# A fourth accumulator in two schemes of seven products, a new order of the products, and six transposes moved behind a branch

## The chip, the cores and the metric

The kernel runs on one core of one Trainium2 chip. The metric is device time in microseconds (us), the median of several executions. The core's engines are named as in the profile: PE (TensorE, matrix products; PEld is its weight loads), DVE (VectorE), ACT (ScalarE), POOL (GpSimd) and SP (SyncE, which starts most transfers). Each works through a queue of its own, and they wait for one another through semaphores.

## The reference

A retention layer over 4 batches, 8 heads, 768 steps and head width 64 gives x, 3072 rows of 512. A router then picks one of 8 experts for each row, and each expert is a two-layer network of its own:

```
state = gamma * state + outer(k_t, v_t);  y_t = scale * q_t @ state        # retention, per batch and head
x     = y as [3072, 512]
logits = x @ w_gate                                                         # [512, 8]
e(row) = argmax(logits);  gate(row) = softmax(logits)[e]
h      = relu(x[rows of e] @ w1[e])                                         # [512, 1024]
out[rows of e] = gate * (h @ w2[e])                                         # [1024, 512]
```

All of it is float32.

## The kernel before, in words

**Stages.** The retention runs first (to about 130 us), in 24 steps of 128 rows. Its output rows are transposed, stored to device memory (`x_d`) and routed on the way. Then come the experts, one after another. The first 256 rows of expert 0 are done ahead of the others, in what is called here the early pair; the rest of expert 0 and experts 1 to 7 are the jobs e = 0 to 7 of the loop at L898. The number of rows n that an expert has is known only at run time, so each job is a switch over 33 unrolled arms, one for each multiple of 8 rows from 256 to 512. An engine enters an arm by a branch and comes back from it by another. PE and ACT get a hint that lets the arm be fetched ahead (`fetch_ahead`, L411).

**Layer 1 of an expert** (`quarters1`, products at L303, for jobs 2 to 7) multiplies w1 and x by a scheme of seven products in place of eight (2 by 2 blocks of w1 and x). It needs four sums of the blocks of w1, S (`halves_of_w1`, four subtractions on POOL at L275, the third of them written over a block of w1 itself), and four sums of the blocks of x, T (`halves_of_x`, four on DVE at L289). A copy of one column of the last T on POOL (L947, `turn_of`) holds POOL's S back until T is made. `quarters1` runs two rounds; a round treats two output blocks f side by side and has seven slots of two products:

- P1 = A11 X11 in `ya`, which ACT copies out to m1 (L315);
- S2 T2 in `yb`; DVE adds m1 and writes u2 (L307);
- S1 T1 in `yc`;
- S3 T3, accumulated on `yb`, so that `yb` holds both; DVE adds m1 and writes u3, then adds u3 to `yc` for one block of h (H11);
- A12 X21 accumulated on `ya`, which ACT turns into the block H00;
- A22 T4 accumulated on `yb`; DVE adds m1 (H10);
- S4 X22 accumulated on `yc`; DVE adds u2 (H01).

A product that accumulates on a bank cannot start before the engine that reads the bank's earlier content has read it.

**Layer 2** of an expert does its rows from 256 on by plain products (`layer2`, L236, two banks of its own, tag "y"), and its first 256 rows by a second scheme of seven (`pair`, products at L349, four matrix instructions each). `pair` uses sums of h, `hs` (`halves_of_h`, DVE, L253 to L256), and sums of w2, `ws` (`halves_of_w`, POOL, L265, done for the next expert during layer 1). Its order is the same: P1 in `ya`, which ACT reads twice (L364) for m10 and m11, with the gates as factors; S2 T2 in `yb`, which DVE reads for u2 (L355); S1 T1 in `yc`; the hint; S3 T3 accumulated on `yb`, which DVE reads for u3; then the part o of `yc`; then the three accumulating products on `ya`, `yb` and `yc`. The last two parts are put off into the next arm (`rest`). In the early pair the operations at L253 and L254 are on DVE and those at L255 and L256 on POOL, and DVE does transposes between its parts (`some`, 4, 7 and 5 of them).

**The banks.** The accumulators of jobs are a fixed list of six banks, `six`; the early pair takes its own by tag. Banks 0 and 1 are `ya` of `quarters1`, 2 and 3 `yb`, 4 and 5 `yc`; `pair` uses 0, 4 and 5; `layer2` alternates between the two banks of tag "y".

**The transposes of x** (`turn`, L209) make the next expert's x ready on DVE: 16 per expert, each of 32 partitions x 512 elements. `quarters1` calls `spare()` between its products, and PLACES says how many transposes each call does. What is left is done after the arm, behind the branch: `turn(xsn, xTn, range(TC), range(sum(PLACES) if e > 1 else 0, Q * Q))`. At job 1 all 16 are there. After it DVE makes T, and POOL, once T is made, makes S, then scatters rows of the output (L392) and gathers those of the expert after next (L166). SP loads w1 and w2 of the expert after next (L150, L155), w2 when the pair is done.

The order on every engine is the order of the code: the experts lie in a manually scheduled region.

## Time and profile before

| what | value |
|---|---|
| median of 3 runs | 480.64 us (478.64 to 481.42) |
| the profiled execution's own time | 479.97 us |
| its span in the profile | 478.2 us |
| mean granted clock of PE | 0.988 of full speed |
| PE busy, instructions | 446.6 us, 3550 |
| DVE busy, instructions | 294.9 us, 666 |
| POOL busy, instructions | 245.8 us, 192 |
| ACT busy, instructions | 130.4 us, 313 |
| early pair, first product at | 151.0 us |
| layer 1 of expert 1, first product at | 178.72 us |
| layer 1 of experts 2 to 7, first product at | 222.74, 264.90, 308.99, 349.94, 393.12, 429.23 us |
| pairs of experts 1 to 7, first product at | 209.01, 251.52, 295.62, 336.01, 379.22, 417.14, 457.49 us |

How to read the views: a line of the timeline has the start in us from the span's start, the length in us, engine, code line, operation, output and inputs by the program's names (banks are `p`, `yp`, `ye`), partitions x elements, and the number of instructions merged. In square brackets stands the engine's idle time before it, and what ended it; "issue" means that the profile shows nothing it waited for. One float32 matrix instruction appears as two rows of PE, so a product of `pair` is 8 rows. A line of the list of waits has the waiting engine and line, the one waited for, us in total, times, and the longest. A line of the stretches has the window, its length, then busy us and instructions of PE, PEld, DVE, ACT and POOL, PE's granted clock, the busy share of the DMA engines, and GB/s moved. Line numbers are those of the kernel before; after the change, lines from 804 on stand one lower.

### The profile page before, as it was taken

How to read it: one execution, taken by the hardware profiler on the slowest of the kernel's cores; microseconds unless marked ns; L12 is line 12 of the kernel's file. 1: busy time of each engine (PE TensorE's matmuls, PEld its weight loads, DVE VectorE, ACT ScalarE, POOL GpSimd, SP SyncE). 2: the span in 40 equal slices, each digit the busy share in tenths (PEclk: the TensorE clock that was granted, in tenths of full speed). 3: DMA queues.
4: the chain of work that ended last, by engine and by line, in shares of the span. 5: the costliest groups of instructions: out<-in, count | busy, mean ns of one | idle time of the engine just before them, and what ended most of it. 6: DMA issues, size and time to landing. Idle time of an engine off the chain costs nothing.

```text
span 478.2 us, 9303 instructions
## 1 busy us (share of the span) xinstructions
PE 446.6 (93%) x3550; PEld 356.2 (74%) x3550; DVE 294.9 (62%) x666; ACT 130.4 (27%) x313; POOL 245.8 (51%) x192
## 2 busy tenths in 40 slices
PE   8999998899799999999999999979999989999992
PEld 4777777677568955558867995779699679689872
DVE  4468768788687892744782694358468638833410
ACT  2454453445222111210231131113113212213310
POOL 2763533440306151759848863890588188089111
PEclk9999998999999999999999999989999999999998
DMA  9999999997831199343613714260562416001001
GB/s 201 226 229 225 216 240 233 211 217 217 268 90 40 33 382 374 125 146 106 235 37 146 269 48 164 83 246 2 180 205 105 162 59 211 5 6 61 3 28 48
DMA packets 93538, 72.71 MB, mean 152 GB/s; under 512 B 53482, under 2 KB 78058, under 8 KB 93424
## 3 DMA queue, kind: packets, MB, share of 16 engines
q1 hardware_dynamic: 88160, 58.74, 43.6%
q0 software_dynamic: 5120, 12.60, 7.4%
q8 instruction: 47, 0.77, 0.7%
q14 instruction: 67, 0.55, 0.3%
q10 hardware_dynamic: 144, 0.05, 0.0%
HBM read 60.88 MB, written 14.68 MB: 158 GB/s over the span
## 4 chain that ended last, share of the span: by engine, by line
PE 79%; DVE 11%; issue 3%; ACT 2%; SPq 1%; DMA 1%; another core or an unknown queue 1%; POOL 0%; POOLq 0%; DVEq 0%; ACTq 0%
PE p L303 23%; PE p L349 15%; PE ye L236 14%; PE p L223 6%; PE y L558 4%; PE sc L526 3%; PE hp L223 3%; PE tr L473 2%; PE yp L349 2%; DVE am L528 2%; PE new L537 2%; PE y L554 1%; PE parts L589 1%; SPq L460 1%; DMA q<-in_q_dram 1%
## 5 line engine op out<-in xcount | busy, mean ns | idle before, releaser
L236 PE MATMUL ye<-w2t,hT 128*8 128x128 f32 (+6 forms) x496 | 66.7, 361 | 0.0
L236 PEld LDWEIGHTS ye<-w2t,hT 128*8 128x8 f32 (+6 forms) x496 | 32.3, 122 | 30.1 <-issue 27.5
L392 POOL DMA_INDIRECT out_dram<-o,dst x30 | 29.9, 997 | 42.5 <-ACT o L244 14.7
L209 DVE STREAM_TRANSPOSE xT<-xs 32x512 f32<-32x512 f32 x64 | 44.9, 702 | 5.8 <-issue 4.7
L166 POOL DMA_INDIRECT xs<-x_d,src x28 | 29.3, 1047 | 29.5 <-DVE gate_e L201 17.1
L349 PE MATMUL p<-ws,hs 128*128 128x256 f32 x168 | 38.7, 382 | 5.3 <-DVE q L355 4.7
L528 DVE TENSOR_TENSOR am<-sc,causal 128x512 f32<-128x512 f32 x48 | 30.7, 682 | 18.5 <-PE sc L526 15.0
L209 DVE STREAM_TRANSPOSE xTs<-xs 32x512 f32<-32x512 f32 x48 | 33.7, 702 | 13.1 <-ACT hT L225 9.1
L303 PE MATMUL p<-t,w1t 128*128 128x196 f32 (+5 forms) x192 | 36.9, 335 | 3.8 <-DVE q L307 3.8
L349 PEld LDWEIGHTS p<-ws,hs 128*128 128x128 f32 x168 | 31.4, 190 | 11.6 <-POOL s L275 2.9
L490 POOL TENSOR_TENSOR vs<-v,dec 128x512 f32<-128x512 f32 x23 | 23.9, 1044 | 28.9 <-PE y L558 12.1
L485 POOL TENSOR_TENSOR qs<-q,dec 128x512 f32<-128x512 f32 x22 | 22.5, 1045 | 29.8 <-DMA q<-in_q_dram 28.8
L303 PEld LDWEIGHTS p<-t,w1t 128*128 128x128 f32 x192 | 32.8, 193 | 4.9 <-DVE q L307 2.7
L947 POOL COPY turn_of<-t 128x1 f32<-128x1 f32 x6 | 1.1, 183 | 68.4 <-DVE t L289 68.4
L355 DVE SCALAR_TENSOR_TENSOR q<-p,gate,q 128x256 f32<-128x256 f32 x14 | 6.8, 483 | 44.9 <-ACT q L364 26.9
L303 PE MATMUL p<-t,s 128*128 128x196 f32 (+5 forms) x192 | 33.8, 329 | 0.0
L265 POOL TENSOR_TENSOR ws<-w2t,ws 128x1024 f32<-128x1024 f32 x14 | 33.0, 2358 | 0.6
L265 POOL TENSOR_TENSOR ws<-w2t 128x1024 f32<-128x1024 f32 x14 | 33.1, 2364 | 0.1
L303 PEld LDWEIGHTS p<-t,s 128*128 128x128 f32 x192 | 32.1, 190 | 0.0
L307 DVE TENSOR_TENSOR hT<-p,q 128x196 f32<-128x196 f32 (+5 forms) x72 | 24.7, 360 | 10.4 <-PE p L303 8.9
L558 PE MATMUL y<-am,vs 128*64 128x128 f32 x384 | 29.3, 283 | 1.5 <-DVE am L528 1.1
L526 PE MATMUL sc<-qT,kT 64*128 64x128 f32 x384 | 28.8, 291 | 0.7 <-ACT kT L511 0.7
(204 smaller groups left out, 851.7 us busy)
## 6 DMA issues: line engine op xcount, KB each, us to landing
w1t<-in_moe_w_dram SPq DMA_DIRECT2D x8, 2048.0 KB, 8.0
w2t<-in_moe_w_dram SPq DMA_DIRECT2D x8, 2048.0 KB, 11.4
k<-in_k_dram SPq DMA_DIRECT2D x24, 256.0 KB, 5.5
v<-in_v_dram SPq DMA_DIRECT2D x24, 256.0 KB, 5.6
x_d<-xg SPq DMA_DIRECT2D x24, 256.0 KB, 4.9
q<-in_q_dram SPq DMA_DIRECT2D x11, 512.0 KB, 5.8
q<-in_q_dram SPq DMA_DIRECT2D x2, 256.0 KB, 3.6
out_dram<-o,dst POOLq DMA_INDIRECT x30, 3.7
```

Of the source, the lines that this page charges most:

```text
L166: nc.gpsimd.indirect_dma_start(out=xs[:, t, :], out_offset=None, in_=x_d[0:rows, :], in_offset=bass.IndirectOffsetOnAxis(ap=idx[:, t : t + ...
L209: nc.vector.transpose(xT[ts(g, L), :, 0 : n * P].rearrange("p a (t r i) -> p r t a i", r=Q, i=L)[:, r, :, :, :], xs[ts(r, L), tiles[0] : t ...
L223: nc.tensor.matmul(hp, lhsT=w1t[:, 0, dt, ts(f, P)], rhs=xT[:, dt, 0:n], start=(dt == 0), stop=(dt == DT - 1))
L236: nc.tensor.matmul(y[j * z : j * z + m, 0:c], lhsT=hT[:, f, t * P + r0 : t * P + r0 + m], rhs=w2t[:, 0, f, ts(j, c)], start=(i == 0), stop ...
L265: by.tensor_tensor(out=ws[i], in0=sums[i][0], in1=sums[i][1], op=ALU.subtract)
L303: nc.tensor.matmul(rows(y), lhsT=a(d, f), rhs=b(d), start=start and d == 0, stop=d == 1, skip_group_check=True)
L307: nc.vector.tensor_tensor(out=to, in0=rows(y), in1=rows(plus), op=ALU.add)
L349: nc.tensor.matmul(y, lhsT=a[:, f, :], rhs=b[:, f, :], start=start and f == 0, stop=f == FH - 1, skip_group_check=True)
L392: done = nc.gpsimd.indirect_dma_start(out=out[:, :], out_offset=bass.IndirectOffsetOnAxis(ap=idx[:, t : t + 1], axis=0), in_=o[:, t, :], i ...
L526: nc.tensor.matmul(sc[j][:, a, :], lhsT=kT[r, a, :], rhs=qT[r, a, :], start=True, stop=True)
L528: nc.vector.tensor_tensor(out=am[j], in0=sc[j], in1=middle(causal[:, :], HP), op=ALU.mult)
L558: nc.tensor.matmul(place_of(a, j), lhsT=vs[:, 2 * a + j, :], rhs=am[j][:, a, :], start=(c == 0), stop=True, skip_group_check=True)
```

## The change

- The list has eight banks now, `acc8`: the two of tag "y" come to it, and `layer2` is handed its bank from them in turn. `quarters1` now has `ya` in 6 and 7, `yb` in 0 and 1, `yc` in 2 and 3, `yd` in 4 and 5; `pair` has `ya`, `yb`, `yc` and `yd` in 4, 5, 2 and 3. The early pair takes a second bank of tag "y".
- Both schemes have a fourth accumulator, `yd`. S3 T3 starts there anew and is no longer added onto `yb`; u3 is then made from `yd` and u2 (in `pair`, from u21), and H10 from `yd` and u2. In `pair` u2 is made twice, once with each gate (u20, u21): six parts on DVE where there were five.
- S3 T3 comes third, ahead of S1 T1, in both schemes, so in the early pair as well. There u20 and u21 also come ahead of the four transposes that stood in front of u2.
- PLACES goes from 14 to 10 transposes per arm, with one `spare()` call moved; six of the sixteen transposes are behind the branch in place of two.

```diff
@@ -1,6 +1,6 @@
 import math
 from contextlib import ExitStack
-from itertools import chain
+from itertools import chain, cycle
 
 import numpy as np
 
@@ -215,21 +215,21 @@
         for _ in turns(xs, xT, tiles, which):
             pass
 
-    six = []
+    acc8 = []
 
     def layer1(n, xT, w1t, hT, f, tags=None):
-        hp = (ps(*tags[f % len(tags)], "hp") if tags else six[2 + f % 4])[:, 0:n]
+        hp = (ps(*tags[f % len(tags)], "hp") if tags else acc8[2 + f % 4])[:, 0:n]
         for dt in range(DT):
             nc.tensor.matmul(hp, lhsT=w1t[:, 0, dt, ts(f, P)], rhs=xT[:, dt, 0:n], start=(dt == 0),
                              stop=(dt == DT - 1))
         nc.scalar.activation(out=hT[:, f, 0:n], in_=hp, func=AF.Relu)
 
-    def layer2(n, hT, w2t, o, t, gate):
+    def layer2(n, hT, w2t, o, t, gate, turn_y):
 
         m = min(n - t * P, P)
         for r0, m in [(P // 2, m - P // 2), (0, P // 2)] if P // 2 < m <= P * 3 // 4 else [(0, m)]:
             parts = 4 if m <= P // 4 else 2 if m <= P // 2 else 1
-            y = ps("y", 2, "ye")
+            y = next(turn_y)
             c, z = DM // parts, P // parts
             for i, f in enumerate((0, 1, 4, 5, 6, 7, 2, 3)):
                 for j in range(parts):
@@ -308,7 +308,7 @@
 
         for f0 in range(0, FH, 2):
             fs = range(f0, f0 + 2)
-            ya, yb, yc = six[0:2], six[2:4], six[4:6]
+            ya, yb, yc, yd = (acc8[i : i + 2] for i in (6, 0, 2, 4))
             m1, u2, u3 = temps
             for i, f in enumerate(fs):
                 product(ya[i], A(0, 0), X(0, 0), f, True)
@@ -317,22 +317,22 @@
             for i, f in enumerate(fs):
                 product(yb[i], Sq(2), Tq(2), f, True)
                 add(rows(u2[i]), yb[i], m1[i])
+            spare()
+            for i, f in enumerate(fs):
+                product(yd[i], Sq(3), Tq(3), f, True)
+                add(rows(u3[i]), yd[i], u2[i])
+            spare()
             for i, f in enumerate(fs):
                 product(yc[i], Sq(1), Tq(1), f, True)
-            spare()
-            for i, f in enumerate(fs):
-                product(yb[i], Sq(3), Tq(3), f, False)
-                add(rows(u3[i]), yb[i], m1[i])
                 add(H(1, 1, f), yc[i], u3[i])
             spare()
             for i, f in enumerate(fs):
                 product(ya[i], A(0, 1), X(1, 0), f, False)
                 nc.scalar.activation(out=H(0, 0, f), in_=rows(ya[i]), func=AF.Relu)
             for i, f in enumerate(fs):
-                product(yb[i], A(1, 1), Tq(4), f, False)
-                add(H(1, 0, f), yb[i], m1[i])
+                product(yd[i], A(1, 1), Tq(4), f, False)
+                add(H(1, 0, f), yd[i], u2[i])
                 nc.scalar.activation(out=hT[:, FH + f, 0:n], in_=hT[:, FH + f, 0:n], func=AF.Relu)
-            spare()
             for i, f in enumerate(fs):
                 product(yc[i], Sq(4), X(1, 1), f, False)
                 add(H(0, 1, f), yc[i], u2[i])
@@ -341,7 +341,7 @@
     def pair(hT, w2t, hs, ws, o, gate, then, tile_of, spare=lambda n: None, tags=None,
              late=False):
 
-        ya, yb, yc = ((ps(*tag, "yp") if tags else six[tag])[:, 0:DH] for tag in tags or (0, 4, 5))
+        ya, yb, yc, yd = ((ps(*tag, "yp") if tags else acc8[tag])[:, 0:DH] for tag in tags or (4, 5, 2, 3))
         g = [gate[:, i : i + 1] for i in range(2)]
 
         def product(y, a, b, start):
@@ -363,27 +363,27 @@
         for i in range(2):
             nc.scalar.activation(out=m1[i], in_=ya, func=AF.Copy, scale=g[i])
         product(yb, S[2], T[2], True)
+        u20, u21 = (part(f"u2{i}", yb, i, m1[i]) for i in range(2))
         spare(4)
-        u2 = part("u2", yb, 0, m1[0])
+        product(yd, S[3], T[3], True)
+        u3 = part("u3", yd, 1, u21)
+        then()
+        spare(7)
         product(yc, S[1], T[1], True)
-        then()
-        product(yb, S[3], T[3], False)
-        spare(7)
-        u3 = part("u3", yb, 1, m1[1])
         part(o[:, 1, DH:DM], yc, 1, u3)
         spare(5)
         product(ya, A(0, 1), B(1, 0), False)
         nc.scalar.activation(out=o[:, 0, 0:DH], in_=ya, func=AF.Copy, scale=g[0])
-        product(yb, A(1, 1), T[4], False)
+        product(yd, A(1, 1), T[4], False)
         if not late:
-            part(o[:, 1, 0:DH], yb, 1, m1[1])
+            part(o[:, 1, 0:DH], yd, 1, u21)
         product(yc, S[4], B(1, 1), False)
         if not late:
-            part(o[:, 0, DH:DM], yc, 0, u2)
+            part(o[:, 0, DH:DM], yc, 0, u20)
 
         def rest():
-            part(o[:, 1, 0:DH], yb, 1, m1[1])
-            part(o[:, 0, DH:DM], yc, 0, u2)
+            part(o[:, 1, 0:DH], yd, 1, u21)
+            part(o[:, 0, DH:DM], yc, 0, u20)
 
         return rest
 
@@ -779,7 +779,7 @@
 
         pair(hTa, wa[1], S, T, oa, egates, lambda: fetch_ahead(which, 0),
              lambda name: att.tile([P, FH * P], F32, tag="v", name=name, bufs=6)[:, 0:DH], some,
-             (("sc", 2), ("sc", 2), ("y", 2)))
+             (("sc", 2), ("sc", 2), ("y", 2), ("y", 2)))
         scatter(oa, targets(*early, "_e"), range(HALF))
         turn(xs2[1], xT1, range(TC))
         dst = targets(inv, far, "")
@@ -800,11 +800,12 @@
 
         first(n)
         tiles = -(-n // P)
+        turn_y = cycle(acc8[6:8])
         order = [tiles - 1] * (tiles > first_tile) + list(range(first_tile, tiles - 1))
         for i, t in enumerate(order):
             if i + 1 == len(order):
                 then()
-            layer2(n, hT, w2t, o, t, gate)
+            layer2(n, hT, w2t, o, t, gate, turn_y)
         if not order:
             then()
 
@@ -860,7 +861,7 @@
                 nc.vector.tensor_tensor(out=val[:, :, i, :], in0=at, in1=inner(told[:, :, i], OV * TC), op=ALU.mult)
             here = mp.tile([P, NT, P], BF16, tag="hT", name="ohere")
             nc.vector.tensor_tensor(out=here, in0=middle(rrow[:, :], NT), in1=inner(prow[:, :], P), op=ALU.is_equal)
-            found = six[5][:, 0 : 5 * OV * TC]
+            found = acc8[5][:, 0 : 5 * OV * TC]
             for n in range(NT):
                 nc.tensor.matmul(found, lhsT=here[:, n, :], rhs=val[:, n, :, :].rearrange("p a s -> p (a s)"),
                                  start=(n == 0), stop=(n == NT - 1))
@@ -878,13 +879,13 @@
             for f in range(FT):
                 layer1(W, xT, w1t, hT, f)
             for t in range(TC):
-                layer2(W, hT, w2t, o2[E % 2], t, ogates[:, ts(j, TC)])
+                layer2(W, hT, w2t, o2[E % 2], t, ogates[:, ts(j, TC)], iter(acc8[6 + t % 2 : 7 + t % 2]))
             scatter(o2[E % 2], odst[:, ts(j, TC)], range(TC))
 
     with tc.manual_schedule(engines={PE, ACT, POOL, DVE, SP}):
         for t in o2:
             nc.gpsimd.memset(t, 0.0)
-        six.extend(ps(tag, n, f"p{i}") for i, (tag, n) in enumerate((("sc", 2), ("sc", 2), ("lg", 1)) + (("tr", 3),) * 3))
+        acc8.extend(ps(tag, n, f"p{i}") for i, (tag, n) in enumerate((("sc", 2), ("sc", 2), ("lg", 1)) + (("tr", 3),) * 3 + (("y", 2),) * 2))
         xT, xTn, rest = xTa, xT1, None
         s3 = [keep2.tile([P, 2, F // 2], F32, tag=f"s{i}", name=f"s{i}", bufs=1) for i in range(3)]
         T = [keep2.tile([P, 2, W // 2], F32, tag=f"t{i}", name=f"t{i}", bufs=1) for i in range(4)]
@@ -892,8 +893,8 @@
         ws = [keep2.tile([P, FH * DH], F32, tag=f"ws{i}", name=f"ws{i}", bufs=1) for i in range(4)]
         temps = [[keep2.tile([P, W // 2], F32, tag=f"q{k}{i}", name=f"q{k}{i}", bufs=1) for i in range(2)] for k in range(3)]
         turn_of = keep2.tile([P, 1], F32, tag="turn_of", name="turn_of", bufs=1)
-        of_pair = dict(m10=temps[0][0], m11=temps[0][1], u2=temps[1][0], u3=temps[2][0])
-        PLACES = (2, 2, 2, 1) * 2
+        of_pair = dict(m10=temps[0][0], m11=temps[0][1], u20=temps[1][0], u21=temps[1][1], u3=temps[2][0])
+        PLACES = (1, 1, 1, 2) * 2
 
         for e in range(E):
             last = e + 1 == E
```

## The prediction

> **What bounds the kernel now.** I read the page first: who is busy, and the chain of work that ended last.
>
> ```profile
> PE 446.6 (93%) x3550; PEld 356.2 (74%) x3550; DVE 294.9 (62%) x666; ACT 130.4 (27%) x313; POOL 245.8 (51%) x192
> ...
> PE 79%; DVE 11%; issue 3%; ACT 2%; SPq 1%; DMA 1%; another core or an unknown queue 1%; POOL 0%; POOLq 0%; DVEq 0%; ACTq 0%
> ```
>
> PE carries the span. The change adds no product and removes none, so it can only fill PE's idle time or make more of it. The second view is therefore the list of waits, PE's rows alone:
>
> ```profile
> PE p L349 <- DVE q L355: 4.7, 5, 1.1
> PE p L303 <- DVE q L307: 3.8, 4, 2.0
> ```
>
> L349 is the product of `pair`, L303 that of `quarters1`: both wait for DVE, nine times. The third view is the timeline of one such wait, in the pair of expert 2:
>
> ```profile
> 251.52 1.89 PE L349 MATMUL p<-w2t,hT 128*128 128x256 f32 x8
> ...
> 253.25 3.62 PE L349 MATMUL p<-ws,hs 128*128 128x256 f32 x16
> ...
> 256.78 0.84 ACT L364 ACTIVATE q<-p,gate 128x256 f32<-128x256 f32 x2 [4.37 <-issue]
> 257.29 0.48 DVE L355 SCALAR_TENSOR_TENSOR q<-p,gate,q 128x256 f32<-128x256 f32 x1 [4.28 <-ACT q L364]
> ...
> 257.92 1.97 PE L349 MATMUL p<-ws,hs 128*128 128x256 f32 x8 [1.06 <-DVE q L355]
> ```
>
> Three products run; the fourth accumulates on `yb`, which DVE must read first, with an operand that ACT, late from the branch, gives at 257.25. The pair of expert 6, where ACT is early, shows the undisturbed length:
>
> ```profile
> 417.14 1.89 PE L349 MATMUL p<-w2t,hT 128*128 128x256 f32 x8
> ...
> 418.87 5.34 PE L349 MATMUL p<-ws,hs 128*128 128x256 f32 x24
> ...
> 429.23 1.54 PE L303 MATMUL p<-xT,w1t 128*128 128x204 f32 x8
> ```
>
> First product to next expert: 12.09 us, 1.73 a product.
>
> **1. The pairs of experts 1 to 5.** By the same two rows they take 13.73, 13.38, 13.37, 13.93 and 13.90 us (209.01 to 222.74, 251.52 to 264.90, 295.62 to 308.99, 336.01 to 349.94, 379.22 to 393.12): 7.9 us above five times 12.09. Of this 1.9 stays: 0.8 at expert 1 (second product waits for the sums of h until 211.50 instead of 210.74), 0.6 at expert 4 (its weight loads wait for ACT 0.20 and 0.46) and 0.5 at expert 5 (the branch, idle 0.38 and a fresh start). The other 6.0 is the wait on `yb`. With `yd` the third product starts a bank of its own and the fourth is on `yc`; neither waits for DVE. What is late next: the fifth product needs ACT's two copies (end 6.10 us after the pair's start at expert 2; the fifth starts at 6.9), and the sixth needs DVE's u3. At expert 2: u20 from 257.29, then u21 and u3 at 0.5 each end by 258.8; the sixth starts at 251.52 + 5 x 1.73 = 260.2. The added DVE operation (six in place of five, 0.48) is in this. At expert 1 the third product now needs the last sum of h (L256, ends 212.68); it starts at 211.50 + 1.73 = 213.23. **-6.0**; ends -4.5 (ACT's return, 4.4 us after its last row, varies: 0.3 of it back at each expert) and -6.2 (only PE's idle times kept).
>
> **2. The six turns behind the branch.** Per expert 2 to 6 four more transposes follow the join: 4 x 0.72 = 2.9 us on DVE, ahead of the four L289 subtractions, POOL's L947 copy and four L275 subtractions, and the pair's own parts. Tightest is expert 4, whose layer 2 is shortest: L289 ends 340.26, now 343.1; u20, u21, u3 end by 344.7; the sixth product comes at 336.01 + 0.6 + 8.65 = 345.3. POOL's third subtraction (w1t, L275) ends 347.56, now 350.4, and the third product of the next layer 1 reads it: 336.01 + 0.6 + 12.09 = 348.7, plus two slots of 1.41, 351.5. It holds by 1.1; at expert 6 (427.19 + 2.9 against 429.23 + 2.8) by 1.9, elsewhere by over 3. So I cost it at nothing. Queued behind on POOL: two scatters, the gathers, the sums of the next w2 (done at 443.95 at expert 7, needed after 457). No DMA is added; gathers and scatters come 2.9 later.
>
> **3. quarters1.** By the chain of waits in order of time, layer 1 of experts 3 and 7 takes 20.07 us at 212 columns and 19.32 at 204: 0.0947 a column in both. At that rate experts 2, 4 and 5 (196, 176, 208 columns) lose 19.77 - 18.56 = 1.2, 21.55 - 16.67 = 4.9 and 20.32 - 19.70 = 0.6: 6.7 together. Expert 4:
>
> ```profile
> 310.26 2.55 PE L303 MATMUL p<-t,s 128*128 128x176 f32 x16
> ...
> 312.82 0.31 ACT L315 COPY q<-p 128x176 f32<-128x176 f32 x1 [2.51 <-PE p L303]
> ...
> 314.28 0.34 DVE L307 TENSOR_TENSOR q<-p,q 128x176 f32<-128x176 f32 x1 [3.39 <-issue]
> ...
> 314.76 0.83 PE L303 MATMUL p<-t,w1t 128*128 128x176 f32 x4 [1.95 <-DVE q L307]
> ```
>
> ACT and DVE are idle, yet start their reads 2 to 3 us after the rows of the products end: the word that a product is done comes late. The stretches of time show this core moving 320 GB/s there, and then:
>
> ```profile
> 312.90:316.30 3.40, 1.01 (x5) 0.78 (x6) 0.88 (x3) 0.22 (x1) 3.07 (x3) 1.00 0.96 320
> 316.40:319.80 3.40, 3.40 (x13) 3.40 (x13) 3.24 (x8) 0.32 (x1) 3.32 (x3) 0.50 0.89 339
> ```
>
> 3.4 us at half clock: 1.7 of expert 4's 4.9. Before, slot four (of seven, 1.4 us each) reads what DVE does with the first half of slot two: 1.5 slots less 0.6, so some 1.5 us of lateness are hidden. After, DVE's first claim is on slot six: u3, after two u2 adds, one transpose and its own add: 3 slots less 1.65, so 2.5 us. With the lateness as it is, expert 4 still waits some 2.4 (its ya, yb, yd and yc end about 314.9, u3 about 317.2) and keeps the half clock; it gains 0.6, experts 2 and 5 half of theirs, 0.9: 1.5 in all. But the lateness follows POOL's gathers (L166), which begin 4.9, 0.5, -2.3 and 2.5 us from the start of layer 1 of experts 2 to 5; with step 2, and pairs 1.2 shorter, they begin about 4 us later, and expert 4 comes to where expert 5 is now (loss 0.6): that gives 4.3 at expert 4 alone. I take **-2.9**, halfway, since neither row is nearer; ends 0 and -6.7. DVE has four transposes fewer in the branch (2.9 us of 20), which helps the same slots.
>
> A rule speaks against a part of this. The Trainium skill, "TensorE: Matmul & The Clock Gate", Part 1 (the clock gate), says that PE's clock falls to half after a whole idle window of about 3.4 us. Expert 4's waits are 1.95 and 0.52, so by the rule the spell is not their doing and stays when they go: its gain of 4.3 would be 2.6, and the sum below 473.2. In the rows the spell follows a stretch with PE busy 1.01 of 3.4 us, and the only earlier one (77.5 to 80.8) one with 1.84 of 3.4; I go by the rows.
>
> **4. The early pair (before the experts).** Here the third product ahead costs something.
>
> ```profile
> 153.18 5.42 PE L349 MATMUL yp<-we,he 128*128 128x256 f32 x24 [0.29 <-DVE he L254]
> ...
> 154.42 1.26 POOL L256 TENSOR_TENSOR he<-hTa 128x512 f32<-128x512 f32 x1
> 155.27 0.48 DVE L355 SCALAR_TENSOR_TENSOR u<-yp,gate_e,m 128x256 f32<-128x256 f32 x1 [0.54 <-PE yp L349]
> ```
>
> POOL makes the last sum of h, done at 155.68; as fourth operand it is wanted at 156.71, as third at 154.98. PE waits 0.75. DVE does worse: the four transposes that now lie at 152.95 to 154.73, in front of u, come behind u20 and u21. From 155.27: two parts 1.0, four transposes 1.8, u3 0.5, seven 3.1, the part of o 0.5, five 2.3, and the last two parts end at about 165.55, where the last L355 row (163.82, 0.48) now ends at 164.30: 1.25 later. Then follow, unmoved, eight small operations and sixteen transposes, which end at 178.5, and layer 1 of expert 1 starts at 178.72. It starts later by **+1.25**; ends +0.75 (PE's wait alone) and +1.5.
>
> **Sum.** -6.0 - 2.9 + 1.25 = -7.65, against the profiled execution's own 479.97 (span 478.2 and 1.8 around it): **472.3**. The 479.97 lies 0.7 below the median of the runs, 480.64; I leave the forecast as it is.
>
> **Rivals.** (a) Only the pairs gain: the late word comes as now and quarters1 returns 1.5 or less. For it: the lateness has its own cause. 479.97 - 6.0 - 1.5 + 1.25 = 473.7; with -4.5 from step 1 and nothing from quarters1, 476.7. (b) The change doesn't do what it says: the wait moves from the fourth to the fifth product, because ACT's copies come later than now. From 0.8 us later on each us costs one; 2 us later at five experts and the 6.0 is gone: 479 to 480. Against it: experts 1 and 6, where ACT came 2.6 us earlier. (c) Slower: the four moved turns, 2.9 us, come onto PE's path at the five joins of experts 2 to 6, over L289, POOL's L275 and the third product: 5 x 2.9 = 14.5, so 479.97 - 6.0 + 1.25 + 14.5 = 489.7. It decides where POOL's third subtraction ends over 1.1 us (expert 4), 1.9 (6) or 3 (others) later than I reckon. Against it: POOL's rows keep 2.34 to 2.37 whatever runs beside them.
>
> **How the numbers follow.** The forecast 0.55, (a) 0.27, (b) 0.08, (c) 0.05, and 0.05 for the unnamed. 0.5% is 2.4 us, about what measuring this kernel can tell from no change; faster means below 478.2. The forecast, (a) and little of the rest are faster: 0.85; (b) mostly the same: 0.09; slower 0.06. Low end: -6.0 - 6.7 + 1.25, 468.5; high end: the 476.7 of (a) and 0.9 for late signals that fall worse (half of what experts 2 and 5 lose now), 477.6.
>
> **What would show it.** The rows PE L349 <- DVE L355 gone, and pairs of 12.1 to 12.7 us; no new row PE <- ACT L364 at the fifth product; layer 1 near 0.0947 a column; the early pair's third product waiting for POOL about 0.7, and layer 1 of expert 1 starting near 180.0; L947 about 2.9 later against the pair. Wrong if PE's L303 waits for POOL L275, or if waits of L303 on L307 grow.

## The result and the profile after

The changed kernel takes 471.95 us (median of 6 runs, 471.41 to 474.16) where the kernel before, beside it, takes 479.87 (477.08 to 482.35): ratio 0.9843, 95% interval 0.9801 to 0.9885 (ratios here are taken over all the runs, so they are not exactly the quotient of the two medians). The forecast was 472.3. The profiled execution of the changed kernel was the slowest of its six: 474.16 us, with a span of 472.4, against 479.97 and 478.2 before.

The list of PE's waits of the changed kernel (total us, times, longest us) has no row of L349 for DVE L355 any more, and less of L303 for L307:

```profile
PE p L303 <- DVE q L307: 1.1, 2, 0.7
...
PE p L303 <- DVE hT L307: 0.7, 1, 0.7
```

The timeline of the pair of expert 2:

```profile
252.35 1.89 PE L349 MATMUL p<-w2t,hT 128*128 128x256 f32 x8
...
254.08 5.34 PE L349 MATMUL p<-ws,hs 128*128 128x256 f32 x24
...
257.66 0.84 ACT L364 ACTIVATE q<-p,gate 128x256 f32<-128x256 f32 x2 [4.42 <-issue]
...
258.17 1.46 DVE L355 SCALAR_TENSOR_TENSOR q<-p,gate,q 128x256 f32<-128x256 f32 x3 [0.45 <-ACT q L364]
...
259.26 1.89 PE L349 MATMUL p<-w2t,hT 128*128 128x256 f32 x8
...
264.44 1.60 PE L303 MATMUL p<-xT,w1t 128*128 128x212 f32 x8
```

ACT is as late as before (4.42), but PE runs through: 264.44 - 252.35 = 12.09 us in place of 13.38. The same subtraction of first rows, for every stage that moved:

| stage, us | before | after |
|---|---|---|
| early pair's start to layer 1 of expert 1 | 27.72 | 28.67 |
| pairs of experts 1, 2, 3, 4, 5 | 13.73, 13.38, 13.37, 13.93, 13.90 | 12.92, 12.09, 12.09, 12.59, 12.99 |
| layer 1 of experts 2, 3, 4, 5 | 19.87, 20.16, 21.54, 20.42 | 19.39, 20.16, 18.23, 20.81 |
| early pair's start to the end of the span | 327.2 | 320.6 |

The pairs give 5.6 us, layer 1 gives 3.4, the early pair takes 0.95; layer 2 takes 1.5 more, and the stages ahead of the early pair 0.8. In the early pair the third product now waits for POOL, as reckoned (timeline):

```profile
155.20 1.26 POOL L256 TENSOR_TENSOR he<-hTa 128x512 f32<-128x512 f32 x1
...
156.51 3.72 PE L349 MATMUL yp<-we,he 128*128 128x256 f32 x16 [0.58 <-POOL he L256]
```

The late word in layer 1 is still there. Expert 4 met it in the first of its rounds before, and meets it in the second now (timeline after):

```profile
317.98 1.36 PE L303 MATMUL p<-t,w1t 128*128 128x176 f32 x8
...
319.62 0.59 DVE L307 TENSOR_TENSOR hT<-p,q 128x176 f32<-128x176 f32 x2 [1.82 <-PE p L303]
...
320.02 1.46 PE L303 MATMUL p<-t,s 128*128 128x176 f32 x8 [0.68 <-DVE hT L307]
```

The spell of half clock that stood at 316.39 before is gone from expert 4. The lateness reaches into layer 2 now. Its first weight loads wait for ACT, which waits for the last sums of DVE (timeline after, expert 4):

```profile
325.75 1.09 DVE L307 TENSOR_TENSOR hT<-p,q 128x176 f32<-128x176 f32 x4
326.12 0.89 ACT L335 ACTIVATE hT<-hT 128x352 f32<-128x352 f32 x2 [3.10 <-DVE hT L307]
...
326.68 0.16 PEld L236 LDWEIGHTS p<-w2t,hT 128*32 128x32 f32 x8 [0.40 <-ACT hT L335]
```

Layer 2 of experts 2, 4 and 5, the ones that met the late word, takes 9.39, 6.03 and 9.42 us, where it took 8.91, 5.48 and 8.86 before (and takes 8.83, 5.49 and 8.86 in the changed kernel on chip B, see below, with no late word): 1.6 of layer 1's 3.4 us come back there.

So far the forecast held. The experiments ran on four other occasions, each on a chip of its own, which I call A, B, C and D. Which chip gave the first result is not on record; "the first chip" below means that occasion, and chip and occasion can't be told apart. On A, B and C the kernel before took 468.9, 468.5 and 468.7 us; on D, 476.95. In no profile of A to C is a late word found. The changed kernel itself ran again on B, and there **it is slower, by 0.5%**. What follows is mostly about that.

### The profile page after: what moved, and what is told of

Its sections match the earlier page's. It is cut to its first block, busy times and chain, and to the rows that moved or that the text cites. A ratio compares the mean times of both kernels' runs of the same rounds, so it can differ in the third digit from the quotient of the medians.

```text
span 472.4 us, 9372 instructions
## 1 busy us (share of the span) xinstructions
PE 447.4 (95%) x3550; PEld 356.0 (75%) x3550; DVE 301.1 (64%) x674; ACT 130.5 (28%) x313; POOL 245.8 (52%) x192
## 4 chain that ended last, share of the span: by engine, by line
PE 77%; DVE 15%; issue 2%; ACT 1%; SPq 1%; DMA 1%; POOL 1%; POOLq 0%; another core or an unknown queue 0%; DVEq 0%; ACTq 0%
PE p L303 21%; PE p L349 17%; PE p L236 12%; PE p L223 5%; PE y L558 4%; PE sc L526 4%; DVE xT L209 4%; PE hp L223 3%; PE tr L473 3%; PE new L537 2%; PE y L554 2%; PE parts L589 2%; DVE am L528 1%; DMA q<-in_q_dram 1%; DVE xTa L209 1%
## 5 line engine op out<-in xcount | busy, mean ns | idle before, releaser
L236 PE MATMUL p<-w2t,hT 128*8 128x128 f32 (+6 forms) x496 | 67.9, 362 | 0.3
L236 PEld LDWEIGHTS p<-w2t,hT 128*8 128x8 f32 (+6 forms) x496 | 31.7, 122 | 32.1 <-issue 27.2
L349 PE MATMUL p<-ws,hs 128*128 128x256 f32 x168 | 37.5, 379 | 0.6 <-DVE hs L254 0.6
L303 PE MATMUL p<-t,w1t 128*128 128x196 f32 (+5 forms) x192 | 36.1, 331 | 1.2 <-DVE q L307 1.1
L303 PE MATMUL p<-t,s 128*128 128x196 f32 (+5 forms) x192 | 35.9, 330 | 0.7 <-DVE hT L307 0.7
L349 PEld LDWEIGHTS p<-ws,hs 128*128 128x128 f32 x168 | 31.8, 190 | 5.3 <-issue 1.0
L948 POOL COPY turn_of<-t 128x1 f32<-128x1 f32 x6 | 1.1, 183 | 64.2 <-DVE t L289 64.2
L307 DVE TENSOR_TENSOR hT<-p,q 128x196 f32<-128x196 f32 (+5 forms) x72 | 23.9, 359 | 16.6 <-PE p L303 13.5
L303 PEld LDWEIGHTS p<-t,w1t 128*128 128x128 f32 x192 | 32.3, 190 | 2.1 <-DVE q L307 2.1
L265 POOL TENSOR_TENSOR ws<-w2t,ws 128x1024 f32<-128x1024 f32 x14 | 33.0, 2358 | 0.6
L265 POOL TENSOR_TENSOR ws<-w2t 128x1024 f32<-128x1024 f32 x14 | 33.1, 2364 | 0.1
L303 PEld LDWEIGHTS p<-t,s 128*128 128x128 f32 x192 | 32.4, 190 | 0.9 <-DVE hT L307 0.9
L558 PE MATMUL y<-am,vs 128*64 128x128 f32 x384 | 30.3, 287 | 2.4 <-DVE am L528 2.2
L307 DVE TENSOR_TENSOR q<-p,q 128x196 f32<-128x196 f32 (+5 forms) x48 | 16.2, 360 | 24.3 <-PE p L303 12.9
L355 DVE SCALAR_TENSOR_TENSOR o<-p,gate,q 128x256 f32<-128x256 f32 x21 | 10.0, 483 | 30.6 <-PE p L349 30.2
```

The source lines that it names most:

```text
L236: nc.tensor.matmul(y[j * z : j * z + m, 0:c], lhsT=hT[:, f, t * P + r0 : t * P + r0 + m], rhs=w2t[:, 0, f, ts(j, c)], start=(i == 0), stop ...
L265: by.tensor_tensor(out=ws[i], in0=sums[i][0], in1=sums[i][1], op=ALU.subtract)
L303: nc.tensor.matmul(rows(y), lhsT=a(d, f), rhs=b(d), start=start and d == 0, stop=d == 1, skip_group_check=True)
L307: nc.vector.tensor_tensor(out=to, in0=rows(y), in1=rows(plus), op=ALU.add)
L349: nc.tensor.matmul(y, lhsT=a[:, f, :], rhs=b[:, f, :], start=start and f == 0, stop=f == FH - 1, skip_group_check=True)
L558: nc.tensor.matmul(place_of(a, j), lhsT=vs[:, 2 * a + j, :], rhs=am[j][:, a, :], start=(c == 0), stop=True, skip_group_check=True)
```

## The experiments

Each time is a median beside the kernel before on the same chip, with the ratio to it and its 95% interval. "From the early pair on" is the span less the start of the early pair, from the profiled execution: what lies ahead of it is the same code in all kernels and differs by up to 4 us from one execution to the next (early pair at 144.9 to 148.8).

| kernel | chip | time, ratio | from the early pair on | pair of expert 4 |
|---|---|---|---|---|
| before, again (before_again) | B | 468.27 (one run) | 321.2 | 15.45 |
| changed, again (after_again) | B | 470.84, 1.0051 (1.003 to 1.0073) | 323.5 | 20.69 |
| x1: fourteen turns in the branch | A | 463.84, 0.9887 (0.9842 to 0.9932) | 315.7 | 12.58 |
| x2: before with the placing alone | A | 472.89, 1.0064 (1.0031 to 1.0097) | 325.6 | 16.49 |
| x3: old pairs | A | 470.81, 1.0043 (1.002 to 1.0066) | 323.5 | 13.18 |
| x4: old quarters1 | A | 470.28, 1.0026 (1.0 to 1.0053) | 322.0 | 19.33 |
| x5: old early pair | B | 469.76, 1.002 (0.9993 to 1.0046) | 322.5 | 20.25 |
| x11: before, w1 loaded late | B | 463.99, 0.9889 (0.9847 to 0.9931) | 315.7 | 13.55 |
| x9: sums of w2 first | C | 463.08, 0.987 (0.9825 to 0.9915) | 315.7 | 12.58 |
| x12: changed, w1 loaded late | C | 466.44, 0.9935 (0.9906 to 0.9963) | 319.7 | 16.42 |
| x15: all that helps | C | 460.69, 0.9822 (0.9787 to 0.9856) | 314.4 | 12.58 |
| x17: before with two moves | D | 470.87, 0.9887 (0.9843 to 0.993) | 319.3 | 12.58 |

### First four: parts undone, or done alone

The expected times of these four were reckoned for the first chip; on A the kernel before takes 11 us less, so stages and ratios are compared.

**x1.** The changed kernel with the old placing:

```diff
-        PLACES = (1, 1, 1, 2) * 2
+        PLACES = (2, 2, 2, 1) * 2
```

> The changed kernel with the turns of x placed as before: fourteen of the sixteen in the branch, two behind it. Theory (fourth accumulator does the work): the pairs of experts 2, 3 and 6 stay at 12.1 us and no L349 waits for DVE L355, so 5.6 us of the gain stay. Layer 1 loses somewhat more than its 3.3 us beside 0.0951 us a column, because scatter and gathers of POOL come 2.9 us earlier and their late stretch falls deeper into layer 1: 4 to 5.5 us lost, time 472.5 to 474.5. Rival (the placing of the turns is what helped layer 1): layer 1 of expert 4 goes back to 20.5 us or more, the 3.4 us are gone, time about 475.5.

Measured: no L349 waits for L355, pairs 12.09 at experts 2, 3 and 6, as the theory says. But layer 1 takes 18.66, 20.16, 16.80 and 19.79 us at experts 2 to 5: at 0.0951 us a column nothing is lost, and both sides' reckoning of a late word has no object here.

**x2.** The kernel before with `PLACES = (1, 1, 1, 2) * 2` and nothing else.

> The kernel before, with one edit: ten of the sixteen turns in the branch, six behind it. Three accumulators and the old order stay. Theory: the pairs keep their wait on yb; it is set by ACT's late copies, the two more transposes ahead of u2 lie in the time in which DVE waits for ACT, so experts 2 to 5 stay at 13.4 to 13.9 us, expert 6 (ACT early) grows by up to 1 us; layer 1 returns at most 1 to 2 of its 6.7 lost us because the late stretch moves by 2.9 us. Time 478 to 481. Rival (placing alone frees layer 1): layer 1 of expert 4 falls from 21.5 to near 18.2 us and the time to 476 to 477.

Measured: L349 waits for L355 six times, 6.9 us. Experts 2, 3 and 5 take 13.34, 13.22 and 14.34, expert 6 13.72 (12.09 in the kernel before), expert 4 16.49. Layer 1 is the same as in x1. The placing alone brings nothing here and costs; more at expert 6 (1.6) than the theory's 1, since u2 waits behind four further turns (six in place of two), not two as the expectation has it.

**x3.** The changed kernel with `pair` as before. Its first accumulator then lies on a bank that the last tile of layer 2 uses:

```diff
-        ya, yb, yc, yd = (... for tag in tags or (4, 5, 2, 3))
+        ya, yb, yc = (... for tag in tags or (6, 2, 3))
```

> The changed kernel with the function pair as before (three accumulators, third product on yc), early pair and those of the experts; quarters1 and the placing stay new. Theory: pairs of experts 1 to 5 back to 13.4 to 13.9 us (13.4 to 14.4 where four transposes ahead of u2 outlast ACT), +5.6 us; layer 1 of expert 1 starts 0.95 us earlier against the early pair; layer 1 as in the changed kernel, 19.4, 20.2, 18.2 and 20.8 us for experts 2 to 5. Time about 476.6 (475.8 to 478.5). Rival (most of the gain is layer 1's): under 474.5.

Measured: this bank brings a wait of its own, of L349 for ACT's L244, 4.7 us in six, and moves the pairs' start 0.94 later (expert 4's 1.7); so its single terms can't be read. Layer 2 and pair together, which hold the move, take 22.33 and 23.96 us at experts 2 and 3, against 20.92 and 22.65 in x1, which has also fewer turns behind the branch: 1.4 and 1.3 us, about what the fourth accumulator gave in the result, but the bank's wait is in them, so this is no separate proof. The total tells nothing, as expert 4 shows next.

**x4.** The changed kernel with the products of `quarters1` in the old order:

```diff
-            ya, yb, yc, yd = (acc8[i : i + 2] for i in (6, 0, 2, 4))
+            ya, yb, yc = acc8[6:8], acc8[0:2], acc8[2:4]
...
+                product(yb[i], Sq(3), Tq(3), f, False)
+                add(rows(u3[i]), yb[i], m1[i])
```

> The changed kernel with the order of quarters1 as before (its fourth product on yb, on banks that the pair's last products do not use); the pair and the placing stay new. Theory (yd lets layer 1 tolerate a late word by one slot more): the L303 waits for DVE L307 come back, experts 2 to 5 lose 5 to 7 us against 0.0951 a column in place of 3.3, time 473.5 to 475.4. Rival (layer 1 gained only because scatter and gathers come later): losses stay at 3 to 3.5 us and the time within 0.7 us of the changed kernel's 472.

Measured: layer 1 of experts 2 to 5 is the same to 0.01 us as in x1. Where no word is late, the old order and the new cost the same, so this run does not tell the two readings of layer 1's gain apart. But the pair of expert 4 takes 19.33 us, and it is the changed kernel's pair. Four kernels of the twelve have that pair at 16.4 to 20.7 us, with PE waiting at the sixth product: x4, x5, x12 and the changed kernel on B. (x2's 16.49 is another case: PE waits 1.98 us at the fourth product, as in the kernel before, behind ACT and the four further turns.)

### The same two kernels on chip B, and two parts

**The changed kernel again.**

> The changed kernel itself, beside the kernel before, on the chip of these runs, where the kernel before takes 468.9 us and not 479.9, and where no kernel shows the late word in layer 1 (expert 4's takes 16.80 us). Theory: with no late word only the pairs and the early pair are left of the change: -5.6 + 0.95, so about 464.2 us, and layer 1 as in the other kernels here (18.67, 20.16, 16.80 and 19.79 us for experts 2 to 5). It holds only if DVE leaves expert 4's branch early; if it leaves over 1 us after the load of w1 is issued, its return takes 4.5 us and not 1.5, and expert 4's pair grows by 5 to 7 us: then 469 to 471. Rival (the quarters' order and the placing bring their part on every chip): 461 or less.

**The kernel before again.**

> The kernel before, for its profile on the chip of these runs. Theory: layer 1 of experts 2 to 5 in 18.67, 20.16, 16.80 and 19.79 us, 6.5 us less than in its first profile; the pairs of experts 2 to 5 at 13.4 to 13.9 with the wait on DVE L355 as they were; the rest of the 11 us ahead of the early pair, which starts near 146 to 148 and not at 151. Rival (the pairs' wait is a thing of the first chip too): pairs of 12.1 here.

Measured: 470.84 for the changed kernel against 468.5. From the early pair on the kernel before has 321.2 us, the changed one 323.5. The pairs of experts 1 to 3 are shorter by 0.92, 1.13 and 1.28, that of 5 by 0.59; from the early pair to layer 1 of expert 1 it takes 1.13 longer (28.85 for 27.72); layer 1 is the same to 0.1; expert 4's pair takes 20.69 in place of 15.45. The case that the expectation set apart, DVE leaving expert 4's branch late, is what came. In the kernel before, layer 1 is 6.5 us shorter than in its first profile and the wait on L355 is there (4.9 us in five), both as expected: the wait belongs to the kernel, the late word to the first occasion.

**x5.** The changed kernel, with the early pair calling the old `pair`.

> The changed kernel with the early pair in its old order (third product on yc, three accumulators); the experts' pairs, quarters1 and the placing stay new. Theory: the wait of yp L349 for POOL's he goes, layer 1 of expert 1 starts 27.7 us after the early pair begins and not 28.7, and 0.95 us are gained against the changed kernel. Rival (DVE's queue, which is free again before layer 1 of expert 1, hides it): the same 28.7 us and no gain.

Measured: 28.03 us from the early pair to layer 1 of expert 1 against 28.85 in the changed kernel on this chip: 0.82 gained, 0.95 expected; the medians differ by 1.08. No slack of DVE hides it. Expert 4's pair stays long (20.25).

**x11.** The kernel before; the load of w1 moves in SyncE's queue:

```diff
-            if e + 2 < E:
-                w1s.append(weights1(homes[e % 2], e + 2))
...
             if e + 2 < E:
                 w2s.append(weights2(homes[e % 2], e + 2))
+                w1s.append(weights1(homes[e % 2], e + 2))
```

> The kernel before with one edit: the load of w1 for the expert after next is issued behind the load of w2 at the end of the job, 12 to 16 us later, not ahead of the pair. Theory (ACT is late from the branch because its first instructions behind it are fetched while the load of w1 moves; where ACT left within 0.7 us of the issue or no load ran it took 1.7 to 2.6 us, else 4.2 to 5.0): ACT's gap at experts 2 to 5 falls to 1.7 to 2.6 us, the wait of L349 for DVE L355 goes or falls under 0.4 us, pairs of experts 2 to 5 at 12.1 to 12.6 us without any fourth accumulator, time 464 to 465. Rival (ACT's return has another cause, as the length of its code): gaps stay at 4.2 to 5.0, pairs at 13.4 to 13.9, time as before.

Measured: as the theory says, with three accumulators. The pair of expert 2, timeline of the kernel before on chip B and then of this one:

```profile
249.56 0.84 ACT L364 ACTIVATE q<-p,gate 128x256 f32<-128x256 f32 x2 [4.21 <-issue]
...
250.69 1.97 PE L349 MATMUL p<-ws,hs 128*128 128x256 f32 x8 [0.89 <-DVE q L355]
```

```profile
249.72 5.34 PE L349 MATMUL p<-ws,hs 128*128 128x256 f32 x24
250.60 0.84 ACT L364 ACTIVATE q<-p,gate 128x256 f32<-128x256 f32 x2 [1.71 <-PE p L349]
...
260.89 0.42 SPq L150 DMA_DIRECT2D w1t<-in_moe_w_dram  x1
```

With the load out of the way ACT is idle 1.71 and not 4.21 us, the third and fourth product run on without a gap (x24), and experts 2, 3 and 5 take 12.09. The time is 463.99, at the low end of the 464 to 465 expected. One edit in another queue gives as much as the fourth accumulator does with fourteen turns in the branch (x1): 315.7 us from the early pair on in both, on B and on A. Expert 4 takes 13.55, since layer 1 behind it starts 0.8 late ("issue"; in the kernel before on B 1.0). The load of w2 is issued 0.7 us ahead of that start; whether it is the cause was not tested.

### Why expert 4's pair takes 20 us

On chip B, the changed kernel. DVE's rows around the join, then POOL's, then PE's:

```profile
318.56 1.75 DVE L253 TENSOR_TENSOR hs<-hT 128x512 f32<-128x512 f32 x1 [0.42 <-ACT hT L339]
320.34 2.73 DVE L254 TENSOR_TENSOR hs<-hs,hT 128x512 f32<-128x512 f32 x1
323.11 0.69 DVE L255 TENSOR_TENSOR hs<-hT,hs 128x512 f32<-128x512 f32 x1
323.72 0.69 DVE L256 TENSOR_TENSOR hs<-hT 128x512 f32<-128x512 f32 x1
329.37 4.29 DVE L209 STREAM_TRANSPOSE xT<-xs 32x512 f32<-32x512 f32 x6 [4.97 <-issue]
```

```profile
317.37 2.38 POOL L265 TENSOR_TENSOR ws<-w2t 128x1024 f32<-128x1024 f32 x1
319.70 2.82 POOL L265 TENSOR_TENSOR ws<-w2t,ws 128x1024 f32<-128x1024 f32 x1
```

```profile
330.58 1.94 PE L349 MATMUL p<-w2t,hT 128*128 128x256 f32 x8
337.91 3.75 PE L349 MATMUL p<-ws,hT 128*128 128x256 f32 x8 [5.40 <-DVE q L355]
```

Read from the top. DVE's sums of h take 1.75 and 2.73 us in place of 0.69, where POOL's sums of w2 (L265) run beside them; each ends some 0.55 us after the L265 that it overlaps. DVE so leaves the branch at 324.40, 1.2 us after the pair's start, where it left 1.5 ahead of it in x1. SyncE issued the load of w1 at 322.49. DVE's next row comes 4.97 us after its leaving, and not 1.5 as in x1. Ten instructions stand ahead of u20 there, four of them the moved turns, and the sixth product waits 5.40 us; then the clock falls to half from 336.0 to 342.8.

Whether DVE or ACT is back soon or late goes by the load of w1 in every profile. Leaving at most 0.8 us after its issue, ahead of it, or with no load, DVE is idle 1.5 to 2.2 us and ACT 1.7 to 2.7; leaving 1.7 to 4.1 us after it, 4.2 to 5.1. The stretch of DMA traffic just behind 324.4 in the changed kernel on B, by queue (packets, MB, share of 16 engines), then the next 1.1 us:

```profile
q1 hardware_dynamic: 273, 1.12, 100.4%
```

```profile
q1 hardware_dynamic: 106, 0.43, 101.3%
q14 instruction: 2, 0.02, 3.6%
```

From 324.4 to 327.3 the engines carry the load and no packet of an instruction queue; from 327.3 to 328.4 two come through, and DVE and ACT start at 329.4 and 329.6. So I read the late return as a fetch of code that waits behind the load. That the load makes it late is tested below and in x11; that it is a fetch rests on these packets, and the view doesn't say for which engine they are.

Two runs take the two links apart.

**x9.** The changed kernel; on POOL the sums of w2 come ahead of the gathers and the scatter:

```diff
-            if e and e + 2 < E:
-                gather(xs2[e % 2], cols[e + 2][0], range(TC))
+            if e == 1:
+                gather(xs2[1], cols[3][0], range(TC))
...
-            if e > 1:
-                scatter(o2[(e - 1) % 2], cols[e - 1][1], [1, 0])
...
             halves_of_w(w2s[e], ws, by=nc.gpsimd)
+            if e > 1:
+                if e + 2 < E:
+                    gather(xs2[e % 2], cols[e + 2][0], range(TC))
+                scatter(o2[(e - 1) % 2], cols[e - 1][1], [1, 0])
```

> The changed kernel with one thing moved on POOL: from expert 2 on the sums of w2 (L265) come ahead of the gathers and the scatter of the job, some 5 to 8 us earlier; the six turns stay behind the branch. Theory (expert 4's pair is long because POOL, 2.9 us later by the moved turns, runs L265 beside DVE's sums of h, which then take 2.73 in place of 0.69 us, so that DVE leaves the branch after the load of w1 is issued): L254 back to 0.69 us at experts 2 to 4, DVE leaves expert 4's branch 1.2 to 1.6 us ahead of the pair, returns in 1.5, the pair takes 12.6 us and not 20.7, time 462.7 (462 to 464). Rival (the turns themselves make DVE late, wherever POOL is): DVE leaves at +1.2 as now, the pair stays near 20, time 470 to 471.

Measured: 463.08, and as the theory says but for DVE's return, 2.20 and not 1.5. DVE's rows at expert 4:

```profile
320.75 0.69 DVE L254 TENSOR_TENSOR hs<-hs,hT 128x512 f32<-128x512 f32 x1
...
322.09 0.68 DVE L256 TENSOR_TENSOR hs<-hT 128x512 f32<-128x512 f32 x1
...
324.98 4.29 DVE L209 STREAM_TRANSPOSE xT<-xs 32x512 f32<-32x512 f32 x6 [2.20 <-issue]
```

The same six turns lie behind the branch and cost nothing: DVE leaves 1.9 us ahead of the pair, which takes 12.58. It is not the turns on DVE that hurt, it is POOL's later sums.

**x12.** The changed kernel with w1's load moved as in x11.

> The changed kernel with the load of w1 issued behind the load of w2 at the end of the job. The collision of L265 with DVE's sums of h stays, so DVE still leaves expert 4's branch about 1.2 us after the pair's start. Theory (the return of 4.97 us is the fetch behind w1's load): DVE returns in 1.5 to 1.7 us, L349 waits about 2.1 for DVE L355 (5.4 less 3.3), the pair takes 14.3 to 15 us in place of 20.7, expert 5's 12.1 in place of 12.7, time 464.5 (463.5 to 466). Rival (DVE's return has another cause): 4.3 to 5.0 and 470 to 471.

Measured: DVE leaves as late as without the edit (1.13 us after the pair's start, L254 at 2.74), and returns in 1.53. The pair takes 16.42, more than the 14.3 to 15 expected, expert 5's 12.74 for 12.1, and the time is 466.44, above the 466:

```profile
325.17 4.29 DVE L209 STREAM_TRANSPOSE xT<-xs 32x512 f32<-32x512 f32 x6 [1.53 <-issue]
```

```profile
329.91 1.89 PE L349 MATMUL p<-w2t,hT 128*128 128x256 f32 x8
333.71 3.45 PE L349 MATMUL p<-ws,hT 128*128 128x256 f32 x8 [1.91 <-DVE q L355]
```

The wait is 1.91, near the 2.1 reckoned; I had left out the half clock, which follows already this idle stretch (3.45 for the eight rows of the product in place of 1.89). So of the 8.1 us that expert 4 loses on B, the collision alone makes 3.8, by C, and the late return on top of it 4.3.

### A better kernel, and one without the change

**x15.** x9's and x11's moves together, the early pair as before, fourteen turns in the branch.

> Meant as the better kernel: the changed one with fourteen turns in the branch as before, the early pair in its old order, the load of w1 behind that of w2, and the sums of w2 ahead of gathers and scatter. Theory: pairs of experts 2 to 6 at 12.1 us (expert 4 at 12.6), expert 1 at 12.9, layer 1 as in the other kernels here, early pair to layer 1 of expert 1 27.7 us; 463.8 of the kernel with fourteen turns, less 1.0 (early pair), 0.9 (branch return of expert 5): 461.9 (461 to 463.5). Rival (moving the transfers makes a wait elsewhere, gathers landing too late for the turns of the next layer 1): 464 or more.

Measured: 460.69, the fastest of all and just below the 461 to 463.5 expected, 0.9822 (0.9787 to 0.9856) of the kernel before. The pairs are as expected but expert 1's, 13.53 (lines 398 and 413 there are 349 and 364 in the others):

```profile
202.12 2.35 POOL L265 TENSOR_TENSOR ws<-w2t,ws 128x1024 f32<-128x1024 f32 x1
203.71 1.30 DVE L253 TENSOR_TENSOR hs<-hT 128x512 f32<-128x512 f32 x1 [8.56 <-ACT o L244]
205.05 0.69 DVE L254 TENSOR_TENSOR hs<-hs,hT 128x512 f32<-128x512 f32 x1
205.88 5.42 PE L398 MATMUL p<-ws,hs 128*128 128x256 f32 x24 [1.21 <-ACT q L413]
```

It is the same collision once more: L253 takes 1.30 beside an L265, and the second product, which needs the sums of h, starts 0.14 us after L254 ends. The profile names ACT's copy, which that product does not read.

**x17.** The kernel before, with x9's and x11's moves and nothing of the change.

> The kernel before, with nothing of the change, and two things moved: the load of w1 behind that of w2 at the end of the job, and the sums of w2 ahead of gathers and scatter on POOL. Theory (with ACT and DVE back from the branch in 1.5 to 2 us, three accumulators are enough where no late word comes): pairs of experts 2, 3, 5 and 6 at 12.1 us and no L349 waiting for DVE L355, expert 4 at 12.6 to 13.6, expert 1 at 13.2 to 13.9; from the early pair's start to the end of the span 314.8 to 315.9 us, time 461 to 463.5, so within 1.5 us of the kernel with all. Rival (the fourth accumulator still earns its part when the return is early): pairs of 12.5 to 13.4, over 317 us from the early pair on, time 464 or more.

This run went to chip D, where the kernel before takes 476.95, so its time stands beside that: 470.87, ratio 0.9887 (0.9843 to 0.993). By the totals, 319.3 us from the early pair on and 470.87, the expectation failed; by the pairs it held: 13.73, then 12.09, 12.09, 12.58, 12.08 and 12.09, with no wait for L355 but expert 1's 0.6. Layer 1 is undisturbed (18.67, 20.16, 16.80, 19.79). Layer 2 is not, and PE itself stalls there in the list of waits:

```profile
PE ye L236 <- issue: 2.6, 4, 1.0
```

Layer 2 of experts 2, 4 and 5 takes 11.66, 6.23 and 10.11 us against 8.84, 5.49 and 8.86 on the other chips: 4.8 us, where layer 1 lost 6.7 in the first profile of before. The moved gathers and scatters run just ahead of these stalls, so it may be the late word, taken along with them; but the stalls are of another kind (PE's own, with "issue", not late reads by ACT and DVE), and no profile of the kernel before was taken on D, so this is not shown. Less the 4.8 it would be 314.5 us from the early pair on, and three accumulators with both moves as good as x15's four (314.4); that is reckoned across two chips, not measured.

## Why the prediction was right, and where it was not

**The sum: near, in part by luck.** The medians fell by 7.9 us for the 7.65 forecast. But the terms, read from the two profiles, add up to 6.6 from the early pair on (-5.6, -3.4, +0.95 and the 1.5 in layer 2, for which the prediction has no term), and the two profiled executions differ by 5.8. And two things that the sum needed were those of the first occasion: the late word, and a step 2 that cost nothing. On B the same change costs 0.5%.

**Step 1, pairs: right.** -5.6 for -6.0. Expert 1 keeps 12.92 for its sums of h, expert 4 12.59, as listed; expert 5 keeps 0.9 and not 0.5 (the branch on PE). Rival (b), a wait at the fifth product for ACT, did not come, with ACT idle as long as 4.82 us (expert 4, chip B). What the step did not ask is why ACT is late. It took 4.4 us as a thing that "varies"; x11 shows that it is the load of w1.

**Step 3, layer 1: right in size there (-3.4 for -2.9), not all of it kept, and no property of the kernel.** With the 1.5 us that layer 2 lost, 1.9 are left. On chip B layer 1 gains nothing: the step's own condition, the late word, is missing on A, B and C. That the lateness follows POOL's indirect transfers was argued there, and x17 fits it without showing it. How much of the 3.4 us came from yd's later claim and how much from the later gathers was not settled: x1 and x4 were to tell it, and ran on a chip with no late word. The half clock went with expert 4's waits in the first profile, as the rows had it. x12's spell of half clock, 3.41 us from 334.03, follows 1.91 us of idle time, and in the 3.41 us ahead of it PE was busy 1.50. The Trainium skill, "TensorE: Matmul & The Clock Gate", Part 1 (the clock gate), asks for a whole idle window of some 3.4 us; the measurement decides against it once more.

**Step 4, early pair: right.** +0.95 on the first chip, +1.13 on B, for +1.25; PE's wait was 0.58 for 0.75, and two parts in a row take 0.88 and not 1.0.

**Step 2, the moved turns: right on the first chip by luck, wrong on A, B and C.** "So I cost it at nothing" holds in the first profile: no L303 waits for L275, though `turn_of` (L948) comes 3.9 us later against expert 2's pair (5.4 us after its start in place of 1.55) and not 2.9. Where it failed is the sentence on what is queued behind on POOL, "the sums of the next w2", which looked at their deadline alone, and the ground given against rival (c), that POOL's rows keep their length "whatever runs beside them": beside DVE's sums they take up to 2.90 (x5). What counted is what runs beside them on DVE: on B it leaves 2.7 us later than in x1, and returns 3.4 later, half clock, 8.1 in all at expert 4. The changed kernel itself ran on B alone; on A (x4) and C (x12), with the same six turns, DVE leaves expert 4's branch as late. So rival (c) is what happens on these chips, at the join that it named first (expert 4), for another reason and at another product: the sixth, for u3, not the next layer's third. A sign of it stood in the trace of before: DVE's L253 at 244.19, 1.08 us long beside an L265, against 0.69. On the first chip expert 4 escaped by little: its layer 1 was 1.4 us longer than on B through the late word, POOL's last L265 (325.32 + 2.38) was done 0.6 us before L254 began, and DVE left 0.5 us ahead of the load of w1, not 1.9 after it:

```profile
327.52 0.73 DVE L253 TENSOR_TENSOR hs<-hT 128x512 f32<-128x512 f32 x1 [0.69 <-ACT hT L339]
328.29 0.69 DVE L254 TENSOR_TENSOR hs<-hs,hT 128x512 f32<-128x512 f32 x1
...
330.81 0.37 SPq L150 DMA_DIRECT2D w1t<-in_moe_w_dram  x1
...
332.00 4.29 DVE L209 STREAM_TRANSPOSE xT<-xs 32x512 f32<-32x512 f32 x6 [1.69 <-issue]
```

The two rows that decide agree with rules of the Trainium skill. "SBUF — State Buffer", Who interferes with whom, says that a DVE instruction with two inputs in SBUF contends with a GpSimd instruction that reads SBUF, at a shared port pair that is an exclusive lock. In the rows L254, starting at 320.34, ends 0.55 us after L265 does (322.52). "Runtime: NRT & Kernel Launch", Instruction fetch mechanics, says that a taken branch to a page that is not at hand has to wait for a DMA fetch. How long the return takes is this case's rows' to say: 1.5 us, and 4.2 to 5.1 behind a load.

## What to carry to other kernels

When a step moves work behind an engine, follow that engine's whole queue, and ask of each row that moves what it now runs beside, not only who waits for it. When a wait ends with an engine that was "late from the branch", ask first what the DMA engines carried then: moving a load in another queue may be the cheaper cure, and x11 needed nothing else. A gain that rests on a margin of 1 or 2 us should be measured on more than one chip or occasion before it is believed: this one was -1.6% on one and +0.5% on another.

## What the runs showed of the hardware

- An engine's return from a branch depends on DMA traffic: 1.5 to 2.7 us without a load or with one issued at most 0.8 us before the engine left, 4.2 to 5.1 when a load of 2 MB was issued 1.7 to 4.1 us before.
- A 128x512 sum of two SBUF operands on DVE takes 0.69 us alone and up to 2.90 beside POOL's 128x1024 sums (x11), which take up to 2.90 in place of 2.36 (x5).
- The same kernel took 468.5 to 479.9 us (medians), by chip or occasion: in the two profiles of before 6.5 us of the difference lie in layer 1, where on the first one ACT and DVE read products 1 to 3 us after their rows end, and 5.7 ahead of the early pair. What differs is not known.
- PE's granted clock fell to half (0.50) after as little as 1.9 us of idle time (x12).
